# Storing the first two row tiles one by one, and moving two small row transfers behind them, in the last stage of an attention-and-spectral-mixing kernel

## The chip, the cores and the metric

The kernel runs on one core of a Trainium2 chip. The metric is the device time of one execution in microseconds (us). Most executions of one kernel agree within 0.3%. A ratio below is the record's; it compares means of the fast runs of the same rounds, so it is not quite the ratio of the medians beside it. The experiments ran in three calls, on three chips (5, 2 and 4 in the record), and each time is set beside runs of the kernel before from the same call. A length read from a profile, such as the tail's, comes from one profile of each kernel.

## The reference, cut to what matters

```python
x = window_attention(q, k, v)                  # 8 batches, 576 rows, 512 columns
X = np.fft.rfft(x, axis=1)                     # first 64 modes mixed by w_r, w_i (64 x 512 x 512 each)
...
y = np.fft.irfft(Y, n=S, axis=1)
u = x + y
return (u + np.maximum(u @ w_ch, 0.0)).astype(np.float32)
```

Until about 390 us the kernel computes attention and streams the mixing weights. The change is in what follows: the inverse transform, the two sums and the stores of the output, 9.44 MB. This document calls that the tail, and counts its length from PE's first product of line 870 to the end of the span.

## The kernel before

The output is made in 36 tiles of 128 rows by 512 columns, here numbered n = 0 to 35. Each goes through PE (products with a trigonometric table), ScalarE (rectifier), PE again and VectorE (final add), and then to memory. One add takes VectorE 0.68 us, and through the tail one ends every 0.68 us on average (34 of them in 23.0 us). The table is multiplied with a tile `Y` per batch. The last eight rows of each batch's `Y` come last, all batches together, in a small tile `yl`. For batches 2 to 7 they must change partitions, so a DMA of 32 KB moves them: this is a "send". PE waits for it when it reaches the batch.

```python
def send(b):
    r0 = 2 * R + RL * (b - 2)
    nc.sync.dma_start(out=batch_tile(b)[128 - RL:].bitcast(FP32), in_=yl[r0:r0 + RL].bitcast(FP32))
...
def finish(n):
    b, t = seq[n]
    add(n, "Yb", True)                                     # PE
    ...
    nc.vector.tensor_tensor(out=ot[:, j], in0=ps, in1=x_sb[:, b, t, :], op=ALU.add)
    if t == NT - 1:
        nc.sync.dma_start(out=out[b:b + 2, 128 * t:, :].rearrange("i s e -> s i e"), in_=ot[:, 0])
    ...
    elif j:                                                # every second tile: a pair, 512 KB
        nc.sync.dma_start(out=out[b, 128 * t - 128:128 * t + 128, :].rearrange("(p j) e -> p j e", j=2),
                          in_=ot)

for n in range(NT):
    rectify(n)
    if n == 2:
        nc.scalar.copy(out=yl[0:NR, 0], in_=psw[0:NR])     # the last piece of the rows to send
send(2)
turn_of = {1: 3, 5: 4, 9: 5, 12: 6, 15: 7}                 # after tile n: send of batch
for n in range(NQ):
    finish(n)
    if n in turn_of:
        send(turn_of[n])
    ...
```

SyncE issues nearly all stores and all sends, in program order.

The softmax here doesn't subtract the row's maximum and nothing guards it: scores larger than these inputs give would overflow.

Of the kernel before, what the change touches and what calls it, by code (L numbers as in the profile page):

```python
# [20 lines left out]
def view(ap, off, dims):  # L21

    return bass.AP(ap.tensor, ap.offset + off, [list(ap.ap[0])] + [list(d) for d in dims])
# [3 lines left out]
def kernel(  # L27
# [10 lines left out]
    nc = tc.nc  # L38
# [110 lines left out]
    with tc.tile_pool(name="tmpf", bufs=1, side="right") as tmp:  # L149
# [8 lines left out]
        for t0, t1 in ((0, 3), (3, NT)):  # L158
            n = t1 - t0
# [232 lines left out]
    with tc.manual_schedule(engines={mybir.EngineType.PE, mybir.EngineType.Pool}):  # L392
# [26 lines left out]
        for w in range(last_unit + 1):  # L419
# [5 lines left out]
            n = len(todo)  # L425
# [146 lines left out]
    with ExitStack() as p2a:  # L572
# [30 lines left out]
        for m in range(L0 * MG):  # L603
            mode(m)
            if m == 8:
                for b in range(1, B, 2):
                    tc.keep_in_program_order(nc.scalar.copy(out=x_sb[64:128, b - 1, NT - 1, :],
                                                            in_=x_sb[64:128, b, NT - 1, :]))
# [8 lines left out]
            if m == Z_M - 2:  # L617

                with tc.tile_pool(name="tmpi", bufs=1, reuse_waits="tile") as tmp:
# [23 lines left out]
                    for tab, row in ((trigI, pcol),):  # L643
# [23 lines left out]
                        for i in range(NT):  # L667
                            n = SW if i < NT - 1 else 64
# [23 lines left out]
    def batch_tile(b):  # L692

        if b not in Yp:
            Yp[b] = wmid.tile([128, 2, DM], FP32R, name=f"Y{b}", tag=f"wm{b}")
        return Yp[b]

    def pair_tile(what, b):

        return batch_tile(b)[:, ("yw", "Yb").index(what), :]  # L700

    def parts_of(b, t):
        return [(b, 0, 128)] if t < NT - 1 else [(b, 0, 64), (b + 1, 64, 64)]
# [5 lines left out]
    def turned(lhs, m, psa, psw):  # L709
        for e in range(NC):  # L710
            nc.tensor.matmul(out=psw[:m, :], lhsT=lhs(e), rhs=wch[:, e, :], start=(e == 0), stop=(e == NC - 1))
        for e in range(NC):
            nc.tensor.transpose(out=psa[:m, e, :], in_=lhs(e), identity=ident_r)
# [21 lines left out]
    NQ = len(seq)  # L735
# [12 lines left out]
    def on_act(n):  # L748
        return n >= len(PLACES) and (seq[n][1] == NT - 1 or n in (11, 16, 19, 25, 30, 33))

    def lay(n):
        ps = tps[n] = bank([128, DM], FP32, "pso8")
        if on_act(n):
            nc.scalar.copy(out=ps, in_=channel_out(tiles.index(seq[n])))
            return
        nc.tensor.matmul(out=ps, lhsT=ident_r, rhs=channel_out(tiles.index(seq[n])), start=True, stop=False,
                         skip_group_check=True)
# [87 lines left out]
    with tc.manual_schedule(engines={mybir.EngineType.PE, mybir.EngineType.Activation, mybir.EngineType.DVE,  # L845
                                     mybir.EngineType.Pool, mybir.EngineType.SP}):
        nc.vector.tensor_copy(out=view(YT2, R - RL, [[NR, NC], [R, 2], [1, RL]]),
                              in_=view(psl, 0, [[RL * B, NC], [RL, 2], [1, RL]]))
        nc.vector.tensor_copy(out=YT2[:, :, 2 * R:], in_=psl[:, :, 2 * RL:])
        psa = ps_a.tile([128, NC, 128], FP32R, name="psa", tag="psa")  # L850
        psw = ps_a.tile([128, DM], FP32, name="psw", tag="psw")
        turned(lambda e: YT2[:, e, 0:NR], NR, psa, psw)
        lay(EARLY_ROWS)
        flat = psa.rearrange("p c e -> p (c e)")
        yl = yp.tile([128, 2, DM], FP32R, name="yl")
# [5 lines that stand above are left out]
        for b in range(2):  # L861
            nc.scalar.copy(out=pair_tile("yw", b)[E0:], in_=psw[R * b:R * b + R])
            nc.vector.tensor_copy(out=pair_tile("Yb", b)[E0:], in_=flat[R * b:R * b + R])
        nc.vector.tensor_copy(out=yl[0:NR, 1], in_=flat[0:NR])

        def add(n, what, stop):
            b, t = seq[n]
            for bb, r0, k in parts_of(b, t):
                tr = 128 * t + (t == NT - 1 and r0 == 0)
                nc.tensor.matmul(out=tps[n], lhsT=trigI[:, tr:tr + 128], rhs=pair_tile(what, bb),  # L870
                                 start=False, stop=stop and r0 + k == 128, skip_group_check=True)

        def rectify(n):
            add(n, "yw", True)
            nc.scalar.activation(out=tps[n], in_=tps[n], func=ACT_F.Relu)  # L875

        ots = {}

        def finish(n):
            b, t = seq[n]  # L880
            add(n, "Yb", True)
            if t % 2 == 0:
                ots[0] = op.tile([128, 2, DM], FP32, name="ot")
            ot, j = ots[0], t % 2
            ps = tps.pop(n)
            if n == NQ - 1:
                to = out[b, 128 * t - 128:128 * t + 128, :].rearrange("(p j) e -> p j e", j=2)
                for c0, queue in ((0, nc.sync), (DM // 2, nc.scalar)):
                    cc = slice(c0, c0 + DM // 2)
                    nc.vector.tensor_tensor(out=ot[:, 1, cc], in0=ps[:, cc], in1=x_sb[:, b, t, cc], op=ALU.add)  # L890
                    queue.dma_start(out=to[:, 1, cc], in_=ot[:, 1, cc])
                return
            nc.vector.tensor_tensor(out=ot[:, j], in0=ps, in1=x_sb[:, b, t, :], op=ALU.add)  # L893
            if t == NT - 1:
                nc.sync.dma_start(out=out[b:b + 2, 128 * t:, :].rearrange("i s e -> s i e"), in_=ot[:, 0])
            elif n == NQ - 2:
                nc.sync.dma_start(out=out[b, 128 * t:128 * t + 256, :].rearrange("(p j) e -> p j e", j=2)[:, 0],
                                  in_=ot[:, 0])
            elif j:
                nc.sync.dma_start(out=out[b, 128 * t - 128:128 * t + 128, :].rearrange("(p j) e -> p j e", j=2),  # L900
                                  in_=ot)

        AHEAD = 3
        for n in range(NT):
            rectify(n)
            if n == 2:
                nc.scalar.copy(out=yl[0:NR, 0], in_=psw[0:NR])
        send(2)
        turn_of = {1: 3, 5: 4, 9: 5, 12: 6, 15: 7}
        for n in range(NQ):  # L910
            finish(n)
            if n in turn_of:
                send(turn_of[n])
            nxt = n + AHEAD + 2
            new = nxt if n and EARLY_ROWS < nxt < NQ else None
            if new and on_act(new):
                lay(new)
            for r in {2: [5]}.get(n, [n + AHEAD] if AHEAD <= n < NQ - AHEAD else []):
                rectify(r)
            if new and not on_act(new):  # L920
                lay(new)
# [30 lines left out]
```

## Time and profile before

| | before |
|---|---|
| time, median of the first 4 runs | 428.38 us (428.15 to 428.43) |
| span in the profile | 426.7 us |
| tail: from the first product of line 870 to the end | 32.0 us (394.67 to 426.67) |
| VectorE's last add ends | 26.1 us into the tail |
| PE waits for sends in the tail | none |

Absolute times are not the best way to compare two profiles here. So I divide the tail from its own start, at 0, 8, 16 and 28 us. In the view of busy windows the columns are: from and to, length, busy us of PE, PEld, DVE, ACT and POOL with counts, the granted clock, the DMA engines' busy share, and GB/s. Before:

```profile
394.67:402.67 8.00, 8.00 (x31) 5.52 (x32) 7.38 (x13) 7.95 (x16) 0.00 (x0) 1.00 0.42 140
402.67:410.67 8.00, 8.00 (x36) 6.37 (x35) 7.49 (x13) 8.00 (x17) 0.00 (x0) 1.00 1.00 392
410.67:422.67 12.00, 8.80 (x36) 6.38 (x34) 9.67 (x17) 8.23 (x17) 0.00 (x0) 0.96 1.00 396
```

GB/s times the length gives what has moved: 1.12 MB in the first 8 us, 3.14 MB in the next 8. PE and ScalarE are busy all the time, and from 8 us on the DMA engines are too.

### The profile page before, as it was taken

Reading aid. Unit: us, or ns where it says so; the run is one execution under the profiler, and the core shown is the slowest. Engines: PE = TensorE matmul, PEld = TensorE weight load, DVE = VectorE, ACT = ScalarE, POOL = GpSimd, SP = SyncE. Lnnn points to the kernel's source line nnn. Section 1 sums busy time; section 2 is a strip of 40 time slices with the busy share of each in tenths; the row PEclk is TensorE's granted clock in tenths of the full one; section 3 lists DMA queues with packets and bytes.
Section 4 is the critical chain, followed back from the end, with each engine's and each line's share of the span. In section 5 each row is a group of like instructions: output and inputs, shape, how many; then the busy total and the mean of one; then the engine's idle time right before and its main releaser. Section 6 shows DMA issues by size and latency. Waiting matters only on the chain.

```text
span 426.7 us, 11631 instructions
## 1 busy us (share of the span) xinstructions
PE 320.8 (75%) x5179; PEld 229.7 (54%) x5190; DVE 178.0 (42%) x375; ACT 165.0 (39%) x292; POOL 89.2 (21%) x171
## 2 busy tenths in 40 slices
PE   6989998999989865322497787887457685498993
PEld 5655765666665665321376666655244452265781
DVE  5566765766673200306333432221113432240994
ACT  4585766866773121001032322222113331130992
POOL 7231231331021321211121121121211122200000
PEclk9999999999995855555588998888558967589997
DMA  7999999999999999999999999999999999994598
GB/s 141 212 213 212 213 212 214 212 214 212 214 213 215 214 214 260 214 214 214 213 214 214 214 213 214 214 213 214 213 214 213 214 214 213 214 212 81 202 392 311
DMA packets 28657, 92.16 MB, mean 216 GB/s; under 512 B 2832, under 2 KB 3088, under 8 KB 28608
## 3 DMA queue, kind: packets, MB, share of 16 engines
q0 software_dynamic: 25344, 81.80, 96.2%
q1 hardware_dynamic: 3120, 9.50, 5.8%
q8 instruction: 40, 0.66, 0.6%
q10 hardware_dynamic: 144, 0.13, 0.1%
q14 instruction: 9, 0.07, 0.0%
HBM read 162.53 MB, written 9.44 MB: 403 GB/s over the span
## 4 chain that ended last, share of the span: by engine, by line
DMA 49%; PE 36%; DVE 8%; issue 4%; ACT 2%; POOL 1%; DVEq 0%; POOLq 0%
DMA wt<-in_moe_w_i_dram 22%; DMA wt<-in_moe_w_r_dram 18%; DMA wy<-in_moe_w_r_dram 9%; PE pso L316 7%; PE pst L218 6%; PE pso L870 4%; PE psv L235 3%; PE psy L563 3%; DVE x_sb L324 3%; PE pss L372 3%; PE pss L272 2%; PE psx L338 2%; PE pss L291 2%; DVE vT L59 2%; PE psz L596 1%
## 5 line engine op out<-in xcount | busy, mean ns | idle before, releaser
L563 PE MATMUL psy<-XQ,wt 128*128 128x16 bf16 x1616 | 61.3, 191 | 73.7 <-DMA wt<-in_moe_w_i_dram 34.7
L563 PEld LDWEIGHTS <-wt 128*128 128x128 bf16 x1616 | 53.0, 103 | 89.6 <-DMA wt<-in_moe_w_i_dram 39.7
L591 DVE CAST xT<-pxt 128x256 fp32r<-128x256 bf16 (+1 forms) x68 | 26.1, 434 | 61.6 <-PE pxt L584 39.7
L598 ACT CAST Z<-psz 128x512 fp32r<-128x512 f32 x36 | 21.1, 586 | 67.5 <-PE psz L596 67.5
L115 POOL DMA_DIRECT2D wt<-in_moe_w_r_dram x54 | 28.9, 536 | 87.3 <-DMA wt<-in_moe_w_r_dram 42.1
L596 PE MATMUL psz<-wch,xT 128*128 128x512 f32 x144 | 46.3, 465 | 0.0
L115 POOL DMA_DIRECT2D wt<-in_moe_w_i_dram x52 | 27.8, 535 | 85.7 <-DMA wt<-in_moe_w_i_dram 49.1
L297 ACT ACTIVATE et<-pss 128x512 bf16<-128x512 f32 x72 | 39.2, 600 | 13.4 <-PE pss L291 13.4
L316 PE MATMUL pso<-vt,et 128*64 128x65 bf16 (+1 forms) x576 | 34.3, 210 | 4.8 <-DVE x_sb L324 4.7
L316 PEld LDWEIGHTS <-et 128*64 128x64 bf16 (+1 forms) x576 | 24.0, 114 | 17.1 <-issue 9.6
L596 PEld LDWEIGHTS psz<-wch,xT 128*128 128x128 f32 x144 | 29.4, 218 | 5.9 <-ACT Z L598 0.3
L324 DVE TENSOR_TENSOR x_sb<-pso,rcp 128x640 bf16<-128x640 f32 x32 | 26.3, 823 | 0.9
L59 DVE CAST x_sb<-psj 128x512 bf16<-128x512 f32 x18 | 12.3, 689 | 26.3 <-PE psj L773 23.4
L870 PE MATMUL pso<-Y,trigI 128*128 128x512 f32 x80 | 23.1, 402 | 0.1
L893 DVE TENSOR_TENSOR ot<-pso,x_sb 128x512 f32<-128x512 f32 x35 | 22.2, 685 | 1.5 <-PE pso L870 1.1
L272 PE MATMUL pss<-band,ident_bf 64*64 64x512 bf16 x136 | 20.7, 414 | 1.5 <-ACT et L297 1.5
L58 ACT CAST YT<-psy 128x256 fp32r<-128x256 f32 x6 | 2.2, 372 | 50.6 <-DVE YT L59 50.6
L59 DVE COPY vT<-pst 128x768 bf16<-128x768 bf16 x16 | 15.3, 958 | 13.0 <-PE pst L218 13.0
L58 ACT CAST x_sb<-psj 128x512 bf16<-128x512 f32 x18 | 10.5, 585 | 25.7 <-PE psj L773 25.7
L59 DVE CAST YT<-psy 128x256 fp32r<-128x256 f32 x6 | 2.5, 425 | 42.9 <-PE psy L563 42.9
L875 ACT ACTIVATE pso<-pso 128x512 f32<-128x512 f32 x36 | 19.2, 596 | 0.0
L870 PEld LDWEIGHTS pso<-Y,trigI 128*128 128x128 f32 x80 | 14.5, 188 | 5.5 <-ACT pso L875 1.7
(160 smaller groups left out, 492.7 us busy)
## 6 DMA issues: line engine op xcount, KB each, us to landing
wt<-in_moe_w_r_dram POOLq DMA_DIRECT2D x54, 512.0 KB, 19.1
wt<-in_moe_w_i_dram POOLq DMA_DIRECT2D x52, 512.0 KB, 19.1
out_dram<-ot SPq DMA_DIRECT2D x15, 512.0 KB, 4.4
rk<-in_k_dram POOLq DMA_DIRECT2D x8, 576.0 KB, 9.8
rq<-in_q_dram POOLq DMA_DIRECT2D x8, 576.0 KB, 13.7
rv<-in_v_dram POOLq DMA_DIRECT2D x8, 576.0 KB, 12.4
wy<-in_moe_w_r_dram POOLq DMA_DIRECT2D x3, 512.0 KB, 17.0
wy<-in_moe_w_i_dram POOLq DMA_DIRECT2D x3, 512.0 KB, 19.1
```

Source lines behind the costliest of these rows:

```text
L59: return nc.vector.tensor_copy(out=o, in_=i)
L115: nc.gpsimd.dma_start(out=wt, in_=src[m].rearrange("(p c) e -> p c e", c=NC))
L218: nc.tensor.transpose(out=ps[64 * hh:64 * hh + 64, c, :], in_=src[:, hh, (c0 + c) * D:(c0 + c + 1) * D], identity=ident_bf)
L272: nc.tensor.matmul(out=pss[(2 * w + hh) % 3][64 * half:64 * half + 64, :], lhsT=ident_bf[pp, pp], rhs=view(band[pp], 128 * half, [[0, WIN ...
L297: nc.scalar.activation(out=et[:, hh, :], in_=pss[(2 * w + hh) % 3], func=ACT_F.Exp, scale=EX_SCALE)
L316: nc.tensor.matmul(out=pso[po, hh, (i // 2) * VW:(i // 2) * VW + D + 1], lhsT=et[pk, hh, col:col + 64], rhs=vt[pk, 1 - f % 2, 2 * hh + g / ...
L324: nc.vector.tensor_tensor(out=view(x_sb, b * NT * DM + g * D, [[4 * D, 2], [DM, NT], [1, D]]), in0=view(pso, 0, [[512, 2], [VW, NT], [1, D]]),
L563: nc.tensor.matmul(out=psy[:, m % MG, e, :], lhsT=w[:, c, 128 * e:128 * e + 128], rhs=XQ[:, c, :, 1 - im:3 - im, m], start=(m % MG == im + ...
L591: nc.vector.tensor_copy(out=xT[:, :, w * k:w * k + w], in_=view(psts[k], j, [[128, NC], [n, w]] if n > 1 else [[128, NC], [1, 64], [64, 2]]))
L596: nc.tensor.matmul(out=psz, lhsT=xT[:, c, :], rhs=wch[:, c, :], start=(c == 0), stop=(c == NC - 1))
L870: nc.tensor.matmul(out=tps[n], lhsT=trigI[:, tr:tr + 128], rhs=pair_tile(what, bb), start=False, stop=stop and r0 + k == 128, skip_group_c ...
L893: nc.vector.tensor_tensor(out=ot[:, j], in0=ps, in1=x_sb[:, b, t, :], op=ALU.add)
```

## The change

The intent is to let store data flow sooner. The first tile is stored alone as soon as it is ready. The send of batch 2 goes between the first and the second store, and the send of batch 3 goes behind the second pair store.

```diff
-            elif n == NQ - 2:
+            elif n in (0, NQ - 2):
                 nc.sync.dma_start(out=out[b, 128 * t:128 * t + 256, :].rearrange("(p j) e -> p j e", j=2)[:, 0],
                                   in_=ot[:, 0])
+            elif n == 1:
+                nc.sync.dma_start(out=out[b, 0:256, :].rearrange("(p j) e -> p j e", j=2)[:, 1], in_=ot[:, 1])
...
-        send(2)
-        turn_of = {1: 3, 5: 4, 9: 5, 12: 6, 15: 7}
+        turn_of = {0: 2, 3: 3, 5: 4, 9: 5, 12: 6, 15: 7}
```

## The prediction

> **What bounds the kernel now.** I read the page first (slices and chain), then the last 35 us in four views: the chain in order of time, the timeline of SyncE's queue, the busy windows of half a microsecond, and the waits. The whole change lies in that stretch: nothing before the last weight tile (389.6 us) is touched, so the first 396 us should stay as they are.
>
> The end of the chain in order of time (columns: start us, duration us, what):
>
> ```profile
> 394.67 2.20 PE pso L870 x7
> ...
> 418.82 1.28 DVE ot L893 x2
> 420.10 0.33 DVEq L947
> 420.43 0.33 DVE ot L890
> ```
>
> Arithmetic ends at 420.8, but the span is 426.7: the last 5.9 us hold only stores. The windows (first to last us, total, busy us of PE, PEld, DVE, ACT, POOL with counts, clock, DMA share, GB/s) show where the stores' data begin and end:
>
> ```profile
> 398.00:398.50 0.50, 0.50 (x2) 0.32 (x3) 0.31 (x2) 0.50 (x2) 0.00 (x0) 1.00 0.00 0
> 398.50:399.00 0.50, 0.50 (x3) 0.42 (x3) 0.50 (x1) 0.50 (x2) 0.00 (x0) 1.00 0.38 49
> 399.00:399.50 0.50, 0.50 (x4) 0.26 (x2) 0.50 (x2) 0.50 (x2) 0.00 (x0) 1.00 0.09 16
> 399.50:400.00 0.50, 0.50 (x4) 0.41 (x3) 0.50 (x2) 0.50 (x2) 0.00 (x0) 1.00 0.99 401
> ...
> 401.00:401.50 0.50, 0.50 (x4) 0.41 (x3) 0.50 (x2) 0.50 (x2) 0.00 (x0) 1.00 0.66 205
> 401.50:402.00 0.50, 0.50 (x4) 0.35 (x3) 0.45 (x1) 0.50 (x2) 0.00 (x0) 1.00 0.73 279
> 402.00:402.50 0.50, 0.50 (x4) 0.45 (x3) 0.45 (x1) 0.50 (x2) 0.00 (x0) 1.00 1.04 418
> ...
> 423.50:424.00 0.50, 0.00 (x0) 0.00 (x0) 0.00 (x0) 0.00 (x0) 0.00 (x0) 0.50 1.00 346
> ```
>
> Look at the last two columns: the DMA engines are idle to 398.8, carry one small send to 399.5, then run near full to 424.3. 9.44 MB are written (page part 3); at the 401 to 418 GB/s of full windows that is 23 us of pure moving. VectorE makes a 256 KB tile every 0.65 us (403 GB/s), so producers and drain run at almost the same rate, and what the stores lost by starting late stays as a backlog. SyncE's timeline (start us, duration us) shows why they start late:
>
> ```profile
> 397.44 0.80 SPq L859 DMA_DIRECT2D Y<-yl  x1
> 398.30 0.73 SPq L900 DMA_DIRECT2D out_dram<-ot  x1
> 399.22 0.68 SPq L859 DMA_DIRECT2D Y<-yl  x1
> 399.95 0.92 SPq L900 DMA_DIRECT2D out_dram<-ot  x2
> ...
> 421.17 1.12 SPq L891 DMA_DIRECT2D out_dram<-ot  x1
> ```
>
> The first tile is ready at 397.10 (the adds start at 396.42 and take 0.68), the second at 397.7, but the first store starts at 398.30: it waits for its pair, and behind the send of batch 2, which itself waited for a ScalarE copy until 397.42. The second store, ready at 399.2, stands behind the send of batch 3 until 399.95.
>
> **What the Trainium skill says.** "DMA: Bandwidth & Descriptors", section "Why a DMA increments its semaphore by 16 and not by 1": a copy is spread over the largest k up to 16 that divides the outer dimensions, the lowest-numbered k engines on this path. So a send of 8 rows uses 8 of the 16 engines, and the trace agrees: a send's semaphore gets one update early and then eight singly (399.51 to 399.93 for the first). Same page, "Queues, rings and completion order": each engine takes its descriptors in ring order. So a send queued behind stores waits for them. The trace agrees: the second send, issued at 399.22 behind a 512 KB store, landed at 402.33 (3.1 us), the first, with nothing ahead, in 2.5 us. Same page, "Latency and other measured facts": the first byte of a DMA on this path comes after about 600 ns. The trace differs: the first store's packets start 1.22 us after the start of its issue instruction, move for 1.28 us, and have landed on all engines at 401.57, 3.27 us after the issue. I use the measured 1.22.
>
> **The change part by part.**
>
> (a) Removed: one pair store (512 KB) behind the first send. Added: two stores of 256 KB, so one more issue on SyncE, 0.5 to 0.7 us by its neighbours. Packets of 2 KB take 85 ns and those of 4 KB 164 ns in the packet records, so halves move no slower. No instruction of PE, ScalarE or VectorE changes; only SyncE's order does (I compared the builds).
>
> (b) Issue times after, from those durations. Tile 0: 397.13 to 397.85. Send of batch 2: 397.9 to 398.65. Tile 1: 398.7 to 399.3. Tiles 2 and 3 (ready 399.2): 399.35 to 399.9. Send of batch 3: 399.95 to 400.65. Tiles 4 and 5: 400.7 to 401.2 (before: 400.43). Send of batch 4: to 401.9. Tiles 6 and 7: 401.98, not moved, as VectorE sets it.
>
> (c) Data, on the eight engines that also carry sends, adding 1.22 us. Tile 0 moves 398.35 to 399.0; the send until 399.9; tile 1 to 400.55; tiles 2 and 3 to 401.85. Now the send of batch 3: in the trace of before, its seven or eight 4 KB packets took 0.8 to 1.07 us each (a store's takes 0.16), all at the same time; this is the half-rate hole of 400.8 to 401.8 above. I keep 0.95: to 402.8. Tiles 4 and 5 to 404.1, the next send to 404.25, tiles 6 and 7 to 405.55. Before, on the same engines: pair 0/1 from 399.52 to 400.8, send to 401.75, pair 2/3 to 403.05, 4/5 to 404.35, send, 6/7 to 405.85. So 1.2 us of earlier start becomes only about 0.3 us at tile 7: the stores are then held by VectorE and by SyncE's issues, and the gap between tile 0 and tile 1 (0.9 us, the first send) is empty for stores.
>
> (d) Does the 0.3 us live to the end? A store without backlog lands in 3.3 us. The thinnest points later: pair 9/10 3.76 us, pair 14/15 3.73, pair 16/17 3.8. So the backlog falls to about 0.45 us there; 0.3 fits under it, more than 0.45 would not. At the end there is more: the last issue at 421.17 could land at 423.2 (1.22 + 0.33 + 0.5) and lands at 425.5, so the end follows the drain, and one slow engine in it (its last packet ends 0.65 us after the others').
>
> (e) The cost: the sends land later. Batch 2 would land near 400.3 (before 399.93); PE needs it at 401.6: free. Batch 3 would land near 403.2 (before 402.33); PE takes it at 403.02: a PE stall of 0 to 0.3 us, passed on to ScalarE (busy 99% there) and VectorE. Late in the tail that is under the backlog of 1.7 us or more; at pair 14/15 and 16/17 it eats a little of the 0.45.
>
> Sum: minus 0.3 us, at most minus 0.45, with a loss of about 0.05 from the stall: 428.36 - 0.3 = 428.05.
>
> **The rivals.**
>
> (1) Full shift: the stores start 1.2 us earlier and the whole drain moves by it; 427.2. For it: the drain looks solid from 402 to 424. Against: the thin points in (d), and windows of 300 to 340 GB/s at 405.5, 408.5 and 410.5, where engines ran dry.
>
> (2) Nothing: the eight engines without sends are already waiting for stores at 405.9 and 411, and if the slow engine is one of them, an earlier start is given back at pair 16/17; 428.35. For it: the dip to 303 GB/s at 410.5 to 411.0. Against: the slow engine is in the later half of the landings up to pair 14/15, where the sends' engines are.
>
> (3) The late send of batch 3 stalls PE by 0.5 us or more, and the tail's producers shift; because the end hangs on the drain it costs 0 to 0.3 us: up to 428.6. For it: 0.7 us of slack before, a delay of nearly 0.9 expected. Against: the backlog at the end.
>
> (4) The extra issue fills SyncE: 25 issues took most of 397.4 to 422.3. Against: the waits view has SyncE waiting for VectorE,
>
> ```profile
> SPq L900 <- DVE ot L893: 6.3, 11, 1.1
> SPq L895 <- DVE ot L893: 2.8, 4, 1.1
> ```
>
> 9.1 us over 15 waits, so one issue more is absorbed by tile 7.
>
> **Range and chances.** The step is a fifth of a per cent at best, while 2% is 8.6 us, more than the 5.9 us behind the last add. So neither faster nor slower by 2% can come from this mechanism; I leave 1% for each for an odd state of the chip. Runs of before spread over 0.25 us. Weighting my sum by 0.45, nothing 0.25, full shift 0.15, late send 0.15, the centre is 428.05; from 427.3 (full shift) to 428.65 (stall passed on) should hold 8 in 10.
>
> **What would show it.** Right: the first store issued near 397.1 and store data from 398.35; the PE, ScalarE and VectorE sequences the same; stores through tile 7 landing about 0.3 us earlier; the last add still at 420.8 or up to 0.3 later; the span's end 0.2 to 0.4 earlier. A wait of PE on a DMA near 403, for the batch-3 rows, would show (e) and rival 3. Wrong: if the end moves by 0.8 or more, (d) undervalued the backlog; if stores 2 to 7 land earlier but pair 16/17 does not, rival 2 holds; if the first store does not start near 397.1, step (b) fails.

## The result

The changed kernel took 428.17 us (428.0 to 429.57, 4 runs) against 428.38 us (428.15 to 428.43, 4 runs). The ratio is 1.0003 with a 95% interval of 0.9982 to 1.0025: the same. One run of 429.57 pulls the mean up; the medians differ by 0.21 us. The profiled span is 426.2 us, 0.45 us shorter, but the tail also began 0.28 us sooner (394.39 instead of 394.67), and no line of the change can reach that far back. What the tail itself gained is 32.00 - 31.84 = 0.16 us.

The chain of the changed kernel in order of time (start us, duration us, what) shows the start of the tail and its last adds:

```profile
394.39 2.20 PE pso L870 x7
...
418.72 1.28 DVE ot L893 x2
420.00 0.33 DVEq L948
420.33 0.33 DVE ot L890
```

Counted from the start of the tail, the last add ends at 26.27 us; before it was 26.09. The producers became 0.18 us slower. SyncE's queue, in its timeline, has the order that was wanted:

```profile
396.85 0.37 SPq L897 DMA_DIRECT2D out_dram<-ot  x1
397.48 0.80 SPq L859 DMA_DIRECT2D Y<-yl  x1
398.34 0.38 SPq L900 DMA_DIRECT2D out_dram<-ot  x1
398.93 0.33 SPq L902 DMA_DIRECT2D out_dram<-ot  x1
399.44 0.67 SPq L859 DMA_DIRECT2D Y<-yl  x1
400.15 0.90 SPq L902 DMA_DIRECT2D out_dram<-ot  x1
```

The first store is issued 2.46 us into the tail instead of 3.63, and pair 2/3 at 4.54 instead of 5.28. Pair 4/5 is at 5.76 in both. Half-microsecond windows of the changed kernel show data from 397.7 on, a gap while the send of batch 2 stands in front, two stretches near 403 and 405.5 us in which the DMA engines were partly idle, and a second hole 14 us into the tail:

```profile
397.50:398.00 0.50, 0.50 (x2) 0.30 (x2) 0.50 (x1) 0.50 (x2) 0.00 (x0) 1.00 0.57 217
398.00:398.50 0.50, 0.50 (x4) 0.31 (x3) 0.31 (x2) 0.50 (x3) 0.00 (x0) 1.00 0.80 307
398.50:399.00 0.50, 0.50 (x4) 0.36 (x2) 0.50 (x2) 0.50 (x2) 0.00 (x0) 1.00 0.43 49
...
403.00:403.50 0.50, 0.50 (x3) 0.38 (x3) 0.50 (x2) 0.50 (x2) 0.00 (x0) 1.00 0.73 262
...
405.00:405.50 0.50, 0.50 (x3) 0.38 (x2) 0.40 (x2) 0.50 (x2) 0.00 (x0) 1.00 0.66 238
405.50:406.00 0.50, 0.50 (x4) 0.41 (x3) 0.50 (x1) 0.48 (x2) 0.00 (x0) 1.00 0.73 287
...
408.00:408.50 0.50, 0.50 (x3) 0.38 (x3) 0.50 (x2) 0.50 (x2) 0.00 (x0) 1.00 1.50 324
408.50:409.00 0.50, 0.50 (x4) 0.38 (x3) 0.50 (x2) 0.50 (x2) 0.00 (x0) 1.00 0.63 188
```

The packet records show the hole at 408.3 us: eight packets of 4 KB, as many as the send of batch 6 has, took 0.54 to 1.11 us, where a store's packet takes 0.16. Before, a hole of this kind lay at 400.8 us, with the send of batch 3. It did not vanish, it moved.

And PE now waits for sends. This is PEld's timeline, with the idle time and its releaser in brackets:

```profile
400.13 0.54 PEld L870 LDWEIGHTS pso<-Y,trigI 128*128 128x128 f32 x3 [0.22 <-DMA Y<-yl]
...
403.07 0.19 PEld L870 LDWEIGHTS pso<-Y,trigI 128*128 128x128 f32 x1 [0.27 <-DMA Y<-yl]
```

The windows of the tail, which answer to those of before, show where the lead went:

```profile
394.39:402.39 8.00, 8.00 (x31) 5.38 (x32) 7.30 (x12) 7.95 (x16) 0.00 (x0) 1.00 0.48 176
402.39:410.39 8.00, 8.00 (x36) 6.26 (x35) 7.34 (x13) 7.93 (x17) 0.00 (x0) 1.00 0.94 349
410.39:422.39 12.00, 8.98 (x37) 6.53 (x35) 9.87 (x17) 8.42 (x17) 0.00 (x0) 1.00 1.02 404
```

After 8 us the changed kernel has moved 1.41 MB against 1.12, a lead of 0.29 MB, or 0.7 us at 400 GB/s. In the next 8 us it moves 2.79 MB against 3.14, and at 16 us it is at 4.20 against 4.26: the lead is gone. The landings in the trace say the same. The last of the sixteen engine updates came sooner than before (from the tail's start) by 0.75 us for pair 2/3, 0.37 for pair 6/7 and 0.48 for pair 11/12, then 0.14 us later for tile 13, 0.14 later for pair 14/15, and 0.11 sooner for the last store.

### The profile page after: what moved, and what is told of

It reads as the page before. It is cut to its first block, busy times and chain, and to the rows that moved or that the text cites. A ratio compares the mean times of both kernels' runs of the same rounds, so it can differ in the third digit from the quotient of the medians.

```text
span 426.2 us, 11644 instructions
## 1 busy us (share of the span) xinstructions
PE 322.9 (76%) x5190; PEld 229.8 (54%) x5190; DVE 178.1 (42%) x375; ACT 165.1 (39%) x292; POOL 89.2 (21%) x171
## 4 chain that ended last, share of the span: by engine, by line
DMA 55%; PE 30%; DVE 7%; issue 4%; ACT 2%; POOL 1%; POOLq 0%; DVEq 0%
DMA wt<-in_moe_w_i_dram 48%; PE pso L316 7%; PE pst L218 6%; DMA wy<-in_moe_w_i_dram 4%; PE pso L870 4%; PE psv L235 3%; DVE x_sb L324 3%; PE pss L372 3%; PE pss L272 2%; DMA wt<-in_moe_w_r_dram 2%; PE psx L338 2%; PE pss L291 2%; DVE vT L59 2%; DVE ot L893 1%; PE pso L756 1%
## 5 line engine op out<-in xcount | busy, mean ns | idle before, releaser
L596 PE MATMUL psz<-wch,xT 128*128 128x512 f32 x144 | 45.1, 455 | 0.0
```

The costliest lines, as they stand in the source:

```text
L596: nc.tensor.matmul(out=psz, lhsT=xT[:, c, :], rhs=wch[:, c, :], start=(c == 0), stop=(c == NC - 1))
```

## The experiments

Twelve kernels were run, each timed in five rounds beside the kernel before. Two theories went into the first eight. **A**: the early gain is given back at tile 13, where the engines run dry because SyncE issues that store late, behind a send. **B**: the drain is one backlog from start to end, and the gain lives to the end. All times "into the tail" are from the profile of each run.

| run | time, median us | before, same rounds | ratio (95%) | tail us | last add, us into the tail |
|---|---|---|---|---|---|
| (before) | | | | 32.00 | 26.09 |
| (changed, first) | 428.17 | 428.38 | 1.0003 (0.9982 to 1.0025) | 31.84 | 26.27 |
| after_again | 428.06 | 428.46 | 0.9990 (0.9977 to 1.0003) | 31.83 | 26.36 |
| split_only | 428.43 | 428.46 | 1.0000 (0.9988 to 1.0012) | 32.08 | 26.09 |
| sends_only | 428.54 | 428.46 | 1.0002 (0.9990 to 1.0014) | 32.32 | 26.62 |
| late_first_pair | 428.99 | 428.46 | 1.0024 (1.0006 to 1.0042) | 32.73 | 26.32 |
| after_pool_sends | 428.26 | 428.33 | 1.0001 (0.9982 to 1.0020) | 31.57 | 26.73 |
| before_pool_sends | 428.67 | 428.33 | 1.0004 (0.9989 to 1.0018) | 32.08 | 27.20 |
| after_no_sends | 427.02 | 428.33 | 0.9965 (0.9949 to 0.9981) | 30.57 | 26.09 |
| after_sends_shifted | 429.01 | 428.33 | 1.0013 (0.9993 to 1.0033) | 32.27 | 26.41 |
| before_no_sends | 426.87 | 428.27 | 0.9967 (0.9955 to 0.9979) | 30.66 | 26.08 |
| after_pool_4to7 | 428.60 | 428.27 | 1.0007 (0.9995 to 1.0019) | 31.77 | 27.02 |
| after_pool_4to7_copy1 | 428.91 | 428.27 | 1.0013 (1.0001 to 1.0025) | 32.22 | 27.37 |
| after_copy1 | 428.16 | 428.27 | 1.0016 (0.9983 to 1.0048) | 31.79 | 26.34 |

**The changed kernel again.** No edit.

> The changed kernel once more, for a tight interval. In its first profile the stores through pair 11/12 landed 0.4 to 0.75 us earlier than before, counted from the start of the tail, but from the store of the ninth-batch-row tile (tile 13) on 0.14 us later, and the end only 0.1 us earlier; the rest of the 0.45 us of the span came from a tail that began 0.28 us sooner by luck. Theory A (the early gain is given back at store 13, where the DMA engines run dry because SyncE issues it late, behind a send): 0 to 0.25 us faster than before. Theory B (the drain is one backlog from start to end, and the gain lives): 0.4 to 0.8 us faster.

Measured: 428.06 us against 428.46. The interval still includes 1. The tail is 31.83 us, 0.17 shorter than before, as in the first profile. So the change is worth about 0.2 us, 0.04%. The two tails of the changed kernel agree to 0.01 us, but of the kernel before there is one profile only, and the times alone do not separate the gain from nothing. B's 0.4 us in the end is not there.

**One part alone: the single stores.**

```diff
-        turn_of = {0: 2, 3: 3, 5: 4, 9: 5, 12: 6, 15: 7}
+        send(2)
+        turn_of = {1: 3, 5: 4, 9: 5, 12: 6, 15: 7}
```

> Only the two single stores, the sends where they were (so the first store again stands behind the send of batch 2, near 398.3). A: no difference from before (within 0.15 us). B: 0 to 0.1 us slower from one more issue, no gain, as the first store's data starts at the same time.

Measured: no difference in time, and the tail 0.08 us longer. The first store was again issued 3.63 us into the tail. Splitting does nothing while the send of batch 2 stands in front.

**The other part alone: the sends moved.** The kernel before, with this edit:

```diff
-        send(2)
-        turn_of = {1: 3, 5: 4, 9: 5, 12: 6, 15: 7}
+        turn_of = {0: 2, 3: 3, 5: 4, 9: 5, 12: 6, 15: 7}
```

> Only the sends moved (batch 2 after the first add, batch 3 behind the second pair store), the first two tiles stored as a pair. The pair 2/3 should be issued 0.6 us sooner, the send of batch 3 about 0.7 us later, so PE should wait for it (0.3 to 0.6 us in the waits view). A: end within 0.15 us of before, VectorE's last add 0.1 to 0.3 us later counted from the start of the tail. B: 0.3 us faster or more because pair 2/3 moves sooner.

Measured: 0.08 us slower by the medians, and a tail 0.32 us longer, more than A had allowed. Pair 2/3 was issued at 4.54 us instead of 5.28, but PE's waits of the stretch (engine, line, releaser; us, times, longest) have

```profile
PEld pso L870 <- DMA Y<-yl: 0.6, 1, 0.6
PE pso L870 <- DMA Y<-yl: 0.2, 1, 0.2
```

and the last add came 0.53 us later. The late send of batch 3 is a cost, and alone it outweighs what pair 2/3 gains. So the parts do not add: 0.08 and 0.32 us longer apart, 0.17 shorter together.

**The opposite: a later start.** The kernel before, with the first pair held back:

```diff
+            elif n == 1:
+                held.append(ot)
             elif j:
                 nc.sync.dma_start(out=out[b, ...], in_=ot)
+                while held:
+                    nc.sync.dma_start(out=out[0, 0:256, :].rearrange("(p j) e -> p j e", j=2), in_=held.pop())
```

> The opposite of the change: the kernel before with the pair 0/1 held back and stored behind pair 2/3, so that the first store is issued about 1.6 us later. A: store data starts 1.6 us later, yet most of it is made up where the engines used to run dry, so the end is 0.2 to 0.9 us later. B: the whole drain moves, the end is 1.3 to 1.7 us later. If even A is too strong and the end does not move at all, the early stretch has nothing to do with the end.

Measured: ratio 1.0024, slower beyond its interval, and a tail 0.73 us longer. The delay turned out smaller than I had written, since both sends moved ahead of it: the first store was issued at 4.54 us, 0.91 later than before. For that delay B would say 0.9 us and A up to that, so this run does not separate the two. It suggests something else: a late start is carried to the end nearly whole (0.73 of 0.91 us in the tail, with 0.23 us of it seen in the last add too; 0.53 us by the medians), while an early start is not. It is no pure delay, though: the sends changed their places as well, and PE waited 0.3 us for one of them.

**The sends on another queue.** In the changed kernel, and in the kernel before:

```diff
-            nc.sync.dma_start(out=batch_tile(b)[128 - RL:]...
+            nc.gpsimd.dma_start(out=batch_tile(b)[128 - RL:]...
```

> The changed kernel with all six sends issued from GpSimd, which is idle in the tail, so that SyncE issues stores only. A: store 13 and pairs 14/15 and 16/17 are no longer held behind sends, PE no longer waits for batch 3's rows, the early gain lives: 0.5 to 1.0 us faster than before. B: the same as the changed kernel (within 0.2 us), as SyncE's order after the start does not matter to a backlog.

> The kernel before (first two tiles as a pair) with all six sends issued from GpSimd. The pair 0/1 can then start near 397.75 instead of 398.3. A: 0.3 to 0.8 us faster than before, 0.1 to 0.4 us slower than the changed kernel with GpSimd sends. B: 0.5 us faster (its start alone).

Measured: both the same as before by their ratios. By the medians the second is 0.34 us slower; its ratio is 1.0004 because one of the runs beside it took 430.41 us. In the profile of the first the tail is 31.57 us, 0.43 shorter than before, but its last add comes 0.64 us later. The holes are gone from the packet records of SyncE's queue, none of whose packets took over 0.4 us (the sends' own packets, now on GpSimd's queue, took up to 0.87), while PE's waits grew:

```profile
PEld pso L870 <- DMA Y<-yl: 0.8, 1, 0.8
PE pso L870 <- DMA Y<-yl: 0.4, 1, 0.4
```

In the second they were 1.3 and 0.9 us. A's promise of 0.5 us or more fell, but not because the drain held the end. In these two profiles the last packet of a store ended 3.10 and 3.09 us after the last add, where it is 4.43 in the kernel before and 4.14 in the changed one: with no send in SyncE's queue the stores kept up with VectorE to the end. What was won there was lost because PE waited for the sends and the last add came 0.64 and 1.11 us later; besides, the span ended 1.75 and 1.79 us after the last packet, against 1.38 to 1.48 in the kernels that issue nothing from GpSimd. Nor does the gain in the tail reach the time: the time of the profiled run exceeds its span by 1.94 us here, and by 1.76 to 1.82 in all kernels whose sends are on SyncE or left out (1.84 in the second, 2.08 with four sends on GpSimd, below). Where that difference lies the profile does not show.

**No sends at all.** The result is wrong in batches 2 to 7. First in the changed kernel, then in the kernel before (where `send(2)` goes too):

```diff
             if n in turn_of:
-                send(turn_of[n])
+                pass
```

> The changed kernel without any send (the result is wrong on purpose in batches 2 to 7). It bounds what the sends cost in all: SyncE's six issues, the half-rate holes and PE's wait. A: 0.6 to 1.2 us faster than before, and no window under 350 GB/s between 402 and 423. B: 0.1 to 0.3 us faster than the changed kernel, the time of 0.2 MB.

> The kernel before without any send (wrong on purpose in batches 2 to 7), to lie beside the changed kernel without sends (427.02 us, tail 30.57 us from PE's first sum of the tail to the end). The first two tiles as a pair can be issued when the second is ready. If the sends are what takes the early gain back, then without them the single stores must keep theirs: this kernel 0.3 to 0.6 us slower than its sibling (tail 30.9 to 31.2). If the gain is given back anyway, because the stores catch up with VectorE, the two are equal within 0.15 us.

Measured: 427.02 and 426.87 us, ratios 0.9965 and 0.9967, tails 30.57 and 30.66. This pair settles what the head start is worth by itself. The windows of the kernel before without sends, then of the changed one without sends:

```profile
394.33:402.33 8.00, 8.00 (x31) 5.52 (x32) 7.39 (x13) 7.95 (x16) 0.00 (x0) 1.00 0.49 195
402.33:410.33 8.00, 8.00 (x36) 6.37 (x35) 7.49 (x13) 8.00 (x17) 0.00 (x0) 1.00 0.96 380
410.33:422.33 12.00, 8.79 (x36) 6.38 (x34) 9.66 (x17) 8.22 (x17) 0.00 (x0) 1.00 0.97 385
```

```profile
394.50:402.50 8.00, 8.00 (x31) 5.52 (x32) 7.37 (x13) 7.95 (x16) 0.00 (x0) 1.00 0.50 196
402.50:410.50 8.00, 8.00 (x36) 6.38 (x35) 7.49 (x13) 8.00 (x17) 0.00 (x0) 1.00 0.96 379
410.50:422.50 12.00, 8.79 (x36) 6.38 (x34) 9.66 (x17) 8.22 (x17) 0.00 (x0) 1.00 0.98 386
```

They are the same to a fiftieth of a megabyte. In the packet records the changed one is ahead by 0.22 MB at 4 us, and at 6 us the two have 0.71 and 0.70 MB. The single stores' head start is caught up within two microseconds, because after it both are fed at VectorE's rate. That is the second outcome of the expectation for the kernel before. I had also expected no window under 350 GB/s without sends; at VectorE's rate there are some, so that part was wrong, but the gain of 1.3 us (expected 0.6 to 1.2) is not the 0.1 to 0.3 us of B.

So the sends, 0.2 MB in all, cost the tail 1.34 us in the kernel before and 1.27 in the changed one: their bytes, their issues on SyncE and all that they hold up, taken together. Moving 0.2 MB at 400 GB/s would take 0.5. A pair store's median from issue to landing falls with them, as the view of DMA issues has it (KB each, us), before and in the changed kernel without sends:

```profile
out_dram<-ot SPq DMA_DIRECT2D x15, 512.0 KB, 4.4
```

```profile
out_dram<-ot SPq DMA_DIRECT2D x14, 512.0 KB, 3.1
```
The change could only ever win back what sends held up at the start: of the 0.44 MB by which the kernel before trails its send-free form at 8 us (1.12 against 1.56, the sends' own bytes counted), it recovers 0.29.

**The sends of batches 6 and 7 one tile later.**

```diff
-        turn_of = {0: 2, 3: 3, 5: 4, 9: 5, 12: 6, 15: 7}
+        turn_of = {0: 2, 3: 3, 5: 4, 9: 5, 13: 6, 16: 7}
```

> The changed kernel with the sends of batches 6 and 7 one tile later (after tiles 13 and 16), so that store 13 is issued ahead of the send of batch 6 and pair 14/15 ahead of that of batch 7. A: store 13 is issued about 0.6 us sooner and lands sooner by that; the end is 0.2 to 0.4 us earlier than in the changed kernel. B: no difference (within 0.15 us).

Measured: 429.01 us, and a tail of 32.27, 0.43 longer than the changed kernel's. Tile 13's store was indeed issued 0.38 us sooner (11.93 us into the tail instead of 12.31), and the end did not follow. Slow packets came with each later send, four of 0.48 to 0.61 us from 409.3 on and five of 0.45 to 0.52 us from 411.3. After 16 us it has moved 4.26 MB (176 GB/s, then 356), as the kernel before has. Why its end is later still is only partly seen: the slowest engine's last update lies 0.8 us behind most of the others', where it is 0.6 in the changed kernel. A as I had put it falls here: it is not SyncE's order at tile 13 that takes the lead back, for with that order mended it is lost all the same. In these runs holes came with the sends wherever they were put.

**Only four sends on GpSimd, and ScalarE's copy one step earlier.** In the changed kernel:

```diff
-            nc.sync.dma_start(out=batch_tile(b)[128 - RL:]...
+            (nc.sync if b < 4 else nc.gpsimd).dma_start(out=batch_tile(b)[128 - RL:]...
```

> The changed kernel with the sends of batches 4 to 7 on GpSimd and those of 2 and 3 on SyncE as they are. With all six on GpSimd PE waited 0.8 us for batch 2's rows; here that wait should be 0.2 to 0.3 as in the changed kernel, and SyncE has no send in front of a store from tile 6 on. If sends in SyncE's order and in the stores' rings take the gain back: tail 31.0 to 31.5 us, 0.5 to 0.9 us faster than before. If only the drain counts: like the changed kernel, 31.8.

and with, besides or alone,

```diff
-            if n == 2:
+            if n == 1:
                 nc.scalar.copy(out=yl[0:NR, 0], in_=psw[0:NR])
```

> The same with ScalarE's copy of the send rows one step earlier (before the third relu), so that the send of batch 2 can follow the first store at once. PE's wait for batch 2's rows should go (0.25 us), against a third relu 0.59 us later, which may hold VectorE's third add. Same as the run without it within 0.2 us if the relu is on the path, 0.2 to 0.4 us faster if not.

> The changed kernel with only that copy one step earlier. PE's waits for sends fall from 0.5 to 0.3 us or less; if they had mattered for the end, the tail shortens from 31.84 by 0.2 us or more; if the drain sets it, within 0.1 us.

Measured: with four sends on GpSimd 428.60 us, tail 31.77, and PE's waits for sends not 0.2 to 0.3 but 1.3 us on PEld in two waits: the sends of batches 4 to 7, now issued early (the first 0.06 us ahead of SyncE's send of batch 2), are in flight together with those that PE needs first. That this is the reason is likely, not shown. With the earlier copy besides, 428.91 us, tail 32.22. Both expectations failed. With the earlier copy alone, 428.16 us (one run of 432.65 spoils its ratio) and a tail of 31.79: PE's waits fell from 0.5 to 0.3 us as expected and the tail by 0.05. That agrees with the end being set by the drain, and not by PE's waits of this size, while the sends are on SyncE.

The distance from the last add to the last packet of a store sorts all fourteen profiles. It is 3.08 to 3.10 us in the two kernels without sends and in the four with sends on GpSimd: there the stores keep up, and a wait of PE that delays the last add delays the end. It is 4.02 to 4.92 us in the other eight, which have all six sends on SyncE: there the drain lags behind, and it sets the end.

No correct version beat the changed kernel clear of noise.

## Why the prediction was right or wrong

The number was right: 428.05 us predicted, 428.17 and 428.06 us measured. To a tenth of a microsecond that is partly luck, since the runs of the changed kernel alone spread from 427.79 to 429.57 us, and its steps hold up unevenly.

**What bounds the kernel.** Right in its main reading: the stores drain to the end, and the last add lies some 4 us ahead of the last packet in both profiles (26.09 and 30.52 us into the tail before, 26.27 and 30.41 after). But I called the loss of a late start a backlog that "stays", and concluded that an earlier start would shorten it. The no-send pair shows that it need not. VectorE's pace, which I took as 0.65 us a tile (403 GB/s), is 0.68 us on average, or 388 GB/s: a little below the 401 to 418 of full windows, so that a drain without sends has time to catch up.

**(a)** Right. PE's, ScalarE's and VectorE's sequences are those of before, and packets of 2 KB went at 85 ns.

**(b)** Right. The first store was predicted 2.46 us into the tail (397.13 less 394.67) and came at 2.46. Tile 1, pair 2/3 and pair 4/5 came 0.1 to 0.3 us sooner than written, pair 6/7 0.17 later. VectorE was not the reason: tile 7 was ready at 7.29 us, as before (7.28), but SyncE was still issuing the send of batch 4, which the change had pushed back (6.79 to 7.43 us).

**(c)** Right in size: 0.3 us sooner for pair 6/7, measured 0.37. In part that is luck, as two parts were mistaken and their errors opposed each other: pair 6/7 was issued late, and a hole was missing. The slow packets of batch 3's send, which I kept at 0.95 us, were not there in the changed kernel: one packet of 0.45 us was left at that place. The hole came back at the send of batch 6. And the 1.22 us from issue to first packet, which I applied to every store, holds a long issue instruction: with nothing in front the first store took 0.87. Its issue lasted 0.37 us instead of 0.73, so from the end of the issue the two took 0.50 and 0.49 us. So whether the trace differs from the 600 ns that I cited depends on where one starts to count.

**(d)** This is the step that failed, in "the backlog falls to about 0.45 us there; 0.3 fits under it". The lead was 0.48 us at pair 11/12 and gone at tile 13, a store that I had not listed among the thin points, though it landed in 3.65 us in the kernel before, less than any that I listed. What showed at the end is 0.16 us of tail, half of what the step carried forward. The mechanism was right in kind (a lead is lost where the engines run out of issued stores), the size was not: between 8 and 16 us the changed kernel moved 349 GB/s where the kernel before moved 392. The backlog at the end was mis-sized too. I wrote 1.7 us or more; from the last add to the last packet the kernel before needs 4.43 us and its form without sends 3.10, so it was 1.3 us.

**(e)** Half wrong. "PE needs it at 401.6: free" put batch 2's first use one group of products late. It was at 400.13, and PE waited 0.22 us. Batch 3's wait was 0.27 us, inside the range given. The last add came 0.18 us later, and as written it did not reach the end.

**The rivals.** (1) The full shift did not happen. (2) The early start given back: this is nearest to the truth, though not for its reason. It named the engines without sends and a starved pair 16/17; without sends the lead is gone at 6 us, when both kernels are fed at VectorE's rate. With sends it is gone by 16 us, and VectorE is not the limit there: the changed kernel had moved 4.20 MB by then, its form without sends 4.60. (3) The stall of PE was real, 0.5 us in two waits, and cost the end little: undoing 0.2 us of it changed the tail by 0.05. (4) SyncE took the extra issue (it makes 27 issues in the tail before, not the 25 that I counted): pair 4/5 was issued at the same place and tile 8 too, with only pair 6/7 between them late.

Where the lead went can be read from windows of one microsecond, though no run separates the causes. Of the 0.34 MB lost between 8 and 16 us, 0.15 fall into the hole (14 to 15 us: 223 GB/s against 371 before). Another 0.09 and 0.08 fall between 8 and 9 us and between 11 and 12, where the DMA engines were busy 0.80 and 0.81 of the time against 1.01 and 1.02. The stores due there, pairs 6/7 and 9/10, had been ready at 7.29 and 9.34 us but were issued at 7.48 and 9.89, each just after SyncE had issued a send. That is the cause which theory A named, at other stores. Before, pair 9/10 stood behind a send as well (ready at 9.27, issued at 10.03), but the engines had more stores queued and did not run dry. In the second profile of the same kernel the slowest send packets of that stretch were milder (up to 0.75 us) and the stretch reached 363 GB/s, but the tail was the same. So the share of each cause stays open. Also open is why the eight packets of a send are slow in one place and not in another.

## What to carry to other kernels

Before starting a drain sooner, ask what feeds it: if the producer's rate is about the drain's, a head start is caught up within a few tiles, while a late start, in the one run that tried it, was carried to the end. Look for what stands inside the stream instead. Here small transfers of 0.2 MB cost 1.3 us, and a run without them told that in one step. Moving them about mostly moved their holes, and putting them on another queue delayed PE, which waits for them. The distance from the producer's last tile to the last packet tells which of the two holds the end.

## What the Trainium skill lacked or had wrong

- "DMA: Bandwidth & Descriptors", section "Latency and other measured facts", gives about 600 ns to the first byte for DMAs issued from SyncE, and does not say from where it counts. Here the first packet came 0.87 us after the start of the issue instruction for a store with nothing in front, 1.22 us for a store behind a send and 1.40 us for a send with nothing in front; from the end of that instruction it was 0.50, 0.49 and 0.60 us.
- Same page, section "Issuing engines are not separate DMA queues", calls the issue time usually small relative to the DMA. It was not for these: each send of 32 KB, 0.08 us of moving at 400 GB/s, occupied SyncE for 0.65 to 0.89 us, and the first send of the kernel before landed 2.5 us after the start of its issue, of which the issue took 0.80.
- No page that I read has a figure for a DMA of 8 rows from one part of the on-chip memory to another beside a stream of stores. Its eight packets of 4 KB could take 0.5 to 1.1 us each, all at once, against 0.16 us for a store's packet, and DMA traffic fell to 188 GB/s meanwhile. "SBUF — State Buffer", section "Door 1: The DMA port swizzle", says that bandwidth depends on how many ports the partitions reach, which would fit rows that all lie close together; no run here tested it.
